# Two attention units in one stretch of TensorE, transposes moved between MLP products, and one fixed list for all operations

## The chip, the cores and the metric

The kernel runs on one core of a Trainium2 chip. The metric is the device time of one execution in microseconds (us), as the median of several runs. Five engines of the core matter: TensorE (PE) multiplies matrices into PSUM, whose banks hold 512 fp32 columns for 128 partitions each; VectorE (DVE), ScalarE (ACT) and GpSimd (POOL) do the arithmetic in between; SyncE (SP) starts the loads and stores. Each engine runs its own list of instructions in order and waits at semaphores for the others.

## The reference

All arrays are fp32: q, k and v of 8 batches, 8 heads, 576 positions and 64 columns; the MLP has 4608 tokens, a model width of 512 and a hidden width of 2048.

```python
scores = scale * np.matmul(q, k.transpose(0, 1, 3, 2))
mask = (rel >= 0) & (rel < window)          # window 128
scores = np.where(mask, scores + bias[None], -1000000000.0)
attn = np.exp(scores - np.max(scores, axis=-1, keepdims=True))
attn = attn / (np.sum(attn, axis=-1, keepdims=True) + 1e-09)
x = np.matmul(attn, v)                      # heads side by side: x is 4608 x 512
h = x @ w_in
P = a[0] + a[1] * h + a[2] * h2 + a[3] * h3
Q = 1.0 + np.abs(b[0]) * np.abs(h) + np.abs(b[1]) * h2
out = (P / (Q + 1e-6)) @ w_out
```

## The kernel before

The 4608 rows are 36 blocks of 128. The attention works on units: one unit is two neighbouring blocks (one in the first two tiles) of one pair of heads. There are 76 units, 8 of them in MLP tile 0 and four in each tile from then on. The MLP works on 18 tiles of 256 tokens and takes the hidden width in chunks of 128, two at a time: up products into a bank h of 512 columns, the rational function on it, down products into two accumulators. Most tiles split each fp32 operand in a high and a low part and multiply three times: `up` (L931) takes w_hi x_hi, w_hi x_lo and w_lo x_hi, `down` (L995) does the same with g_h and g_l.

One unit goes through these steps. `scores` (L537) multiplies queries with keys on quarters of the PE array, 14 products for two usual blocks, into the banks sc0 and sc1 (L552). `softmax` folds the band (L561, DVE), adds the bias and takes the maximum (L568, DVE), and takes the exponential (L573, ACT); `shares` scales by the sum (L585, POOL). Then the weights are transposed on PE, copied to p_all, masked to the two triangles by two selects on POOL (`spread`, L607, L619), and multiplied with v (`quarters`, L641, L650; L742 in the other form). The values come in two halves, into the banks px and py. `sum_halves` (L652) copies the first to x (ACT, L385) and adds the second (DVE, L663); x is cast to x_hi (ACT) and x_lo = x - x_hi is formed (POOL or DVE, L665).

A usual unit has one stretch on PE, made in `attention` (L667): the transposes of the unit before it, in eight halves of 64 rows on parts of the array (`turn_halves`, L593, L598), its own scores, and the values of the unit two before it. `hold`, `pair` and `last_pair` (L758, L778, L809) put two units in one stretch from unit PAIRED on; PAIRED is 76 here, so they are not reached, and the last two units take `turn_alone` (L621, with L591) and the values of L742.

The order of all instructions comes from a planner written in Python. `plan.op` notes an operation with its due time, its cost on each engine that could run it, what it reads and writes. `order` (L182) is a list scheduler over these: it places the ready operation with the earliest due time, with estimated costs (`place`, L249). The list FIRST fixes the order (and by an added 10000 the engine POOL or DVE where there is a choice) of the first 1370 operations. Constants such as ML and ME shift the due times of the down products and of the rational function against the up products. Semaphores are then put in from what the instructions read and write.

Of the kernel before, what the change touches and what calls it, by code (L numbers as in the profile page):

```python
# [140 lines left out]


class Op:
    __slots__ = ("rank", "due", "engines", "emit", "deps", "slots", "left", "users", "start", "end", "engine", "after", "follows", "rows", "sb")
# [985 lines left out]
```

## Time and profile before

| | |
|---|---|
| median of 3 runs | 992.52 us (992.27 to 992.98) |
| the profiled execution | 995.22 us |
| its span, first to last instruction | 993.5 us |
| PE busy | 986.2 us (99%) |
| DVE busy | 769.0 us (77%) |
| ACT busy | 690.6 us (70%) |
| POOL busy | 549.7 us (55%) |
| mean granted clock of PE | 0.997 |

The span is what the profiler saw of the one execution; the 1.7 us beside it lie before its first and after its last instruction. A busy share is the time in which an engine had at least one instruction under way, over the span. Products on PE overlap: one of 512 columns lasts some 0.40 us from its start to its end, while the next begins 0.23 us after it, so the cost of a product in the list is the distance of the starts, not its duration. Line numbers are those of the kernel before.

### The profile page before, as it was taken

Reading aid. Unit: us, or ns where it says so; the run is one execution under the profiler, and the core shown is the slowest. Engines: PE = TensorE matmul, PEld = TensorE weight load, DVE = VectorE, ACT = ScalarE, POOL = GpSimd, SP = SyncE. Lnnn points to the kernel's source line nnn. Section 1 sums busy time; section 2 is a strip of 40 time slices with the busy share of each in tenths; the row PEclk is TensorE's granted clock in tenths of the full one; section 3 lists DMA queues with packets and bytes.
Section 4 is the critical chain, followed back from the end, with each engine's and each line's share of the span. In section 5 each row is a group of like instructions: output and inputs, shape, how many; then the busy total and the mean of one; then the engine's idle time right before and its main releaser. Section 6 shows DMA issues by size and latency. Waiting matters only on the chain.

```text
span 993.5 us, 24565 instructions
## 1 busy us (share of the span) xinstructions
PE 986.2 (99%) x9429; PEld 862.6 (87%) x9431; DVE 769.0 (77%) x1843; ACT 690.6 (70%) x1717; POOL 549.7 (55%) x662
## 2 busy tenths in 40 slices
PE   8999999999999999999999999999999999999998
PEld 5767888888989888898898898988899889898997
DVE  4999988877777877777777877777777777777675
ACT  5999776676767666767667767767666767766563
POOL 3799965555545554545564545455554545454332
PEclk8999999999999999999999999999999999999999
DMA  8973312111212111112111211111111111000000
GB/s 263 342 257 110 105 43 74 44 65 49 71 49 71 44 44 63 56 44 65 54 45 46 74 46 51 66 44 66 53 44 64 55 44 59 37 10 23 1 22 22
DMA packets 45140, 69.08 MB, mean 70 GB/s; under 512 B 4448, under 2 KB 29664, under 8 KB 45024
## 3 DMA queue, kind: packets, MB, share of 16 engines
q1 hardware_dynamic: 44736, 67.26, 20.3%
q8 instruction: 74, 1.21, 0.5%
q14 instruction: 42, 0.34, 0.1%
q10 hardware_dynamic: 288, 0.26, 0.1%
HBM read 58.07 MB, written 9.44 MB: 68 GB/s over the span
## 4 chain that ended last, share of the span: by engine, by line
PE 98%; DMA 1%; SPq 1%; DVE 0%; issue 0%; ACT 0%; ACTq 0%
PE h L931 42%; PE acc L995 42%; PE sc L552 6%; PE px L650 4%; PE px L598 2%; DMA kq<-in_kqv 1%; PE py L650 1%; PE px L742 1%; PE pt L591 0%; PE warm L1051 0%; PE h L937 0%; SPq L486 0%; SPq L844 0%; SPq L487 0%; PE sc L598 0%
## 5 line engine op out<-in xcount | busy, mean ns | idle before, releaser
L931 PE MATMUL h<-x_hi,wi_hi 128*128 128x256 f32 x1024 | 290.9, 284 | 0.0
L931 PE MATMUL h<-x_lo,wi_hi 128*128 128x256 f32 x1024 | 287.9, 281 | 0.0
L931 PE MATMUL h<-x_hi,w_lo 128*128 128x256 f32 x1024 | 287.5, 281 | 0.0
L960 POOL TENSOR_SCALAR g_q<-g_u,babs 128x512 f32<-128x512 f32 x142 | 110.1, 775 | 247.1 <-ACT g_u L959 243.1
L931 PEld LDWEIGHTS h<-x_lo,wi_hi 128*128 128x128 f32 x1024 | 192.6, 188 | 36.3
L995 PE MATMUL acc<-wo_hi,g_h 128*128 128x512 f32 x548 | 220.2, 402 | 0.0
L995 PE MATMUL acc<-w_lo,g_h 128*128 128x512 f32 x548 | 216.3, 395 | 0.0
L931 PEld LDWEIGHTS h<-x_hi,wi_hi 128*128 128x128 f32 x1024 | 193.1, 189 | 23.2 <-issue 1.4
L995 PE MATMUL acc<-wo_hi,g_l 128*128 128x512 f32 x548 | 206.7, 395 | 0.0
L931 PEld LDWEIGHTS h<-x_hi,w_lo 128*128 128x128 f32 x1024 | 193.7, 189 | 0.0
L962 POOL TENSOR_TENSOR g_q<-g_q,g_u 128x512 f32<-128x512 f32 x143 | 185.1, 1295 | 13.8 <-DVE g_q L960 2.9
L965 ACT ACTIVATE g_u<-g_q,guard 128x512 f32<-128x512 f32 x144 | 104.4, 725 | 103.7 <-POOL g_q L962 102.2
L963 DVE TENSOR_TENSOR g_p<-h,g_p 128x512 f32<-128x512 f32 x144 | 99.5, 691 | 90.4 <-ACT g_p L961 88.7
L968 DVE SCALAR_TENSOR_TENSOR g_q<-g_q,h 128x512 f32<-128x512 f32 x144 | 98.7, 685 | 68.3 <-ACT h L967 68.0
L959 ACT ACTIVATE g_u<-h 128x512 f32<-128x512 f32 x141 | 83.9, 595 | 95.8 <-PE h L931 95.7
L619 POOL TENSOR_SCALAR_AFFINE_SELECT p_all<-p_all 128x512 f32<-128x512 f32 (+1 forms) x144 | 90.6, 629 | 69.7 <-ACT p_all L385 61.7
L573 ACT ACTIVATE pr<-pr,st 128x128 f32<-128x128 f32 x288 | 114.7, 403 | 8.1 <-DVE st L568 7.8
L961 ACT ACTIVATE g_p<-h,na 128x512 f32<-128x512 f32 x140 | 108.7, 776 | 0.9 <-PE h L931 0.9
L977 DVE TENSOR_TENSOR g_l<-h,g_h 128x512 fp32r<-128x512 f32 x137 | 93.8, 685 | 19.9 <-ACT g_h L385 19.5
L995 PEld LDWEIGHTS acc<-wo_hi,g_h 128*128 128x128 f32 x548 | 103.2, 188 | 6.2 <-issue 0.7
L964 DVE SCALAR_TENSOR_TENSOR g_p<-g_p,na,h 128x512 f32<-128x512 f32 x144 | 106.8, 742 | 1.8
L969 DVE SCALAR_TENSOR_TENSOR h<-g_p,na,h 128x512 f32<-128x512 f32 x144 | 107.9, 749 | 0.0
(110 smaller groups left out, 1800.2 us busy)
## 6 DMA issues: line engine op xcount, KB each, us to landing
kq<-in_kqv SPq DMA_DIRECT2D x68, 320.0 KB, 3.2
v<-in_kqv SPq DMA_DIRECT2D x68, 192.0 KB, 2.4
out<-o SPq DMA_DIRECT2D x34, 256.0 KB, 2.0
raw_w<-in_w_in SPq DMA_DIRECT2D x16, 512.0 KB, 6.3
raw_w<-in_w_out SPq DMA_DIRECT2D x16, 512.0 KB, 5.2
bias_t<-in_bias SPq DMA_DIRECT2D x44, 64.0 KB, 2.9
kq<-in_kqv SPq DMA_DIRECT2D x4, 192.0 KB, 5.5
kq_first<-in_kqv SPq DMA_DIRECT2D x4, 128.0 KB, 3.0
```

What stands on the lines that cost most here:

```text
L573: nc.scalar.activation(ap(pr)[:, y, :], ap(pr)[:, y, :], AF.Exp, bias=ap(st)[:, y : y + 1], scale=-1.0, accum_out=ap(st)[:, 4 + y : 5 + y])
L931: nc.tensor.matmul(h(i), w[:, k, :], x[:, k, :], start=(k == 0 and m == 0), stop=(k == NKC - 1 and m == len(seq) - 1))
L960: plan.op(E, {"g": tsc, "v": dve(W / 2, 1)} if soon else {"g": tsc}, lambda e: eng[e].tensor_scalar(v(g_q), v(g_u), ap(babs)[:, 1:2], ap(b ...
L961: plan.op(E, either(soon, act(W, 1, 2) - 20, dve(W, 2)), lambda e: nc.scalar.activation(v(g_p), v(h_s), AF.Identity, bias=ap(na)[:, 2:3], ...
L962: plan.op(E, {"g": ttc, "v": dve(W)} if soon else {"g": ttc}, lambda e: eng[e].tensor_tensor(v(g_q), v(g_q), v(g_u), ALU.mult), reads=[(g_ ...
L963: plan.op(E, {"v": dve(W)}, lambda e: nc.vector.tensor_tensor(v(g_p), v(h_s), v(g_p), ALU.mult), reads=[(h_s, 0), (g_p, 0)], writes=[(g_p, ...
L964: plan.op(E, {"v": dve(W, 1)}, lambda e: stt(v(g_p), v(g_p), ap(na)[:, 1:2], v(h_s), ALU.add, ALU.mult), reads=[(h_s, 0), (g_p, 0)], write ...
L965: plan.op(E, {"a": act(W, 0, 1)}, lambda e: nc.scalar.activation(v(g_u), v(g_q), AF.Ln, bias=guard, scale=1.0), reads=[(g_q, 0)], writes=[ ...
L968: plan.op(E, {"v": dve(W)}, lambda e: stt(v(g_q), v(g_q), GUARD, v(h_s), ALU.add, ALU.mult), reads=[(g_q, 0), (h_s, 0)], writes=[(g_q, 0)])
L969: plan.op(E, {"v": dve(W, 1)}, lambda e: stt(v(h_s), v(g_p), ap(na)[:, 0:1], v(h_s), ALU.add, ALU.mult), reads=[(g_p, 0), (h_s, 0)], write ...
L977: plan.op(E, {"v": dve(W)}, lambda e: nc.vector.tensor_tensor(v(g_l), v(h_s), v(g_h).bitcast(F32), ALU.subtract), reads=[(h_s, 0), (g_h, 0 ...
L995: nc.tensor.matmul(ap(accs[n][i]), x[:, sl], w, start=(c == c0 and part == 0 and m == 0), stop=(c == c1 - 1 and (part == 1 or plain) and m ...
```

## The change

PAIRED goes from 76 to 20: from the first unit of the fifth tile on, the 56 units that are left are taken two by two. `pair` makes one stretch of PE for two units. It begins with the values of the two units of the pair before (`emit` in `hold`), into two whole banks px and py, then come the scores of the first unit into sc0 and sc1, as ever, then those of the second (`scores_beside`). These have no bank of their own: four of the fourteen products go to the last quarter of sc0 and sc1, and ten into px and py, after the values there were taken out (`take`: copy of px by ACT or DVE, add of py by DVE, for one unit each). The new argument `glue` holds PE in the planner until the second part of the stretch has followed the first. The transposes of a pair are eight whole ones, an operation of their own (`turn_pair`), and x_hi and x_lo are formed for both units at once (`split` in `hold`, 512 columns). FIRST now names all 6242 operations, so that the due times no longer decide anything; some of the constants are changed as well. The up products of the later tiles wait for the whole x of a tile, as those of the first ones did (`x_reads`).

```diff
-    605, 589, 789, 888, 809, 10855, 856, 810, 606, 791, 788, 793, 811, 10876, 1005, 1351, 812, 10889, 592, 10593, 1007, 10878,
-    890, 1017, 790, 813, 1013, 1010, 891, 792, 816, 910, 1018, 814, 879, 892, 911, 1025, 912, 943, 913, 815, 914, 1019,
...
+    605, 589, 789, 888, 809, 10855, 856, 810, 606, 791, 788, 793, 811, 10876, 1005, 812, 10889, 592, 10593, 1007, 10878, 890,
+    1017, 790, 813, 1013, 1010, 891, 792, 816, 910, 1018, 814, 879, 892, 911, 1025, 912, 943, 913, 815, 914, 1019, 11009,
...
+    6205, 6228, 6230, 6232, 6206, 6229, 6234, 6236, 6235, 6231, 6233, 6238, 6237, 6240, 6239, 6241,
...
+        if glue:
+            glue.glue = o
+            o.deps.add(glue)
...
-                        if r[0] <= t and r[3].engine is None and (best is None or (r[1], r[2]) < (best[1], best[2])) and can(r[3], e, t):
+                        if r[0] <= t and r[3].engine is None and (e != "p" or bound in (None, r[3])) and (best is None or (r[1], r[2]) < (best[1], best[2])) and can(r[3], e, t):
...
-    SA, SG, LL, ML, ZA, ME = 0.082, 0, 6.123, 22.844, 0.779, -17.957
-    OE, CL, CO, WL, SI, SO = -7.408, 4.4, 6.342, -5.815, 31.193, -2.944
-    SL, AW, BL, E0, E1, E2 = -9.614, 22.396, 14.524, 24.893, 13.935, 57.569
+    SA, SG, LL, ML, ZA, ME = 0.082, 0, 6.123, 21.3, 0.779, -24.907
+    OE, CL, CO, WL, SI, SO = -6.174, 4.4, 6.342, -5.815, 31.193, -2.944
+    SL, AW, BL, E0, E1, E2 = -9.614, 41.193, -0.448, 24.893, 13.935, 57.569
...
-    PAIRED, PA, PT, PD, TO, TL, EO, SO2 = 76, -0.35, 6.0, 3.0, 0.0, 0.1, 0.0, 0.0
+    PAIRED, PA, PT, PD, TO, TL, EO, SO2 = 20, -0.205, 1.755, 3.0, 6.604, -4.183, 2.082, 20.604
...
+                part = lambda bank, i, y=y: ap(bank)[:, (2 * y + i) * P : (2 * y + i + 1) * P]
+                c.quarters(lambda i: part(px, i), lambda i: part(py, i))
...
+        def take(at, y):
+            cols = slice(2 * P * y, 2 * P * y + 2 * P)
+            plan.op(at + 0.3, {"a": act(2 * P, 1), "v": dve(2 * P)}, lambda e, y=y: copy(e, ap(x)[:, cols], ap(px)[:, cols]), reads=[(px, y)], writes=[(x, y)], follows=follows)
+            plan.op(at + 0.3, {"v": dve(2 * P)}, lambda e, y=y: nc.vector.tensor_tensor(ap(x)[:, cols], ap(py)[:, cols], ap(x)[:, cols], ALU.add), reads=[(py, y), (x, y)], writes=[(x, y)])
+
+        def split(at):
+            b0 = (STARTS[held[0].j] - MSTART[t]) * P
+            into = lambda y: ap(y)[:, p : p + 2, b0 : b0 + 2 * P]
+            both = lambda: ap(x).rearrange("q (y c) -> q y c", y=2)
+            home = lambda y: [(y, (p + i, held[0].j)) for i in range(2)]
+            mine = [(x, 0), (x, 1)]
+            plan.op(at + 0.4, {"a": act(4 * P, 0), "v": dve(2 * P)}, lambda e: copy(e, into(xh), both()), reads=mine, writes=home(xh), sb=True)
+            plan.op(at + 0.5, {"v": dve(4 * P), "g": 190 + 2.08 * 4 * P}, lambda e: eng[e].tensor_tensor(into(xl), both(), into(xh).bitcast(F32), ALU.subtract), reads=mine + home(xh), writes=home(xl), sb=True)
...
+    def scores_beside(c, sc, late):
+        bank = lambda h: ap(sc[2 + h])
+        spare = lambda h: ap(sc[h])[:, 3 * P :]
+        for i in range(c.m):
...
+                if late == (i == 1 and (n == 1 or c.kinds[i] == 1)):
+                    continue
...
+                            to, k0, k1 = bank(h)[q, : 3 * Q], own - Q, own + P
...
+                        nc.tensor.matmul(to, c.qt(i)[r, q], c.kt(k0, k1)[r], start=True, stop=True, tile_position=(64 * h, Q * half))
...
+    def turn_pair(at):
+        if turning:
+            turning.pop().turn_alone(at, "sc0")
+            return
+        both = pairs[-1]
+        reads = [k for c in both for k in c.turned()]
+        pt = [slot(ps1, [P, 4 * P], F32, "pt", tag=f"sc{y}") for y in range(2)]
+        plan.op(at, {"p": 876}, lambda e: [c.turn([lambda k=k, y=y: ap(pt[y])[:, k * P : (k + 1) * P] for k in range(c.n)]) for y, c in enumerate(both)], reads=reads, writes=[(x, 0) for x in pt])
+        for y, c in enumerate(both):
+            c.spread(at + SO2, pt[y])
...
+        px, py = slot(ps3, [P, 4 * P], F32, "px", tag="h"), slot(ps1, [P, 4 * P], F32, "py", tag="ptx")
+        sc = [slot(ps1, [P, 4 * P], F32, f"sc{k}", tag=f"sc{k}") for k in range(2)] + [px, py]
+        emit, reads, writes, take, split = hold(px, py)
...
+        first = plan.op(A, {"p": 2250}, lambda e: [emit(), both[0].scores(sc[:2]), scores_beside(both[1], sc, False)], reads=reads, writes=writes + [(x, k) for x in sc[:2] for k in range(2)], rows=0.5)
+        first.deps.add(stage[a - 1][0])
+        take(A - 3, 0)
+        o = plan.op(A, {"p": 750}, lambda e: scores_beside(both[1], sc, True), reads=both[1].kq_keys, writes=[(px, 0), (py, 0)], rows=0.5, glue=first)
+        take(A + EO, 1)
+        split(A + EO)
...
-            x_reads = lambda k: x_keys(xs[t], t, range(NKC) if n < EARLY else (k,))
+            x_reads = lambda k: x_keys(xs[t], t, range(NKC) if n < EARLY or first_unit[t] >= PAIRED else (k,))
```

Three places show how the lists of the engines differ. The first is PE where a unit begins, in the list before (x_hi, x_lo and w_lo belong to an up product of the MLP, px, sc0 and sc1 are banks, pr holds a unit's weights, id_sb the identity).

```order
L931 MATMUL h_6223<-x_lo_5038,wi_hi_596 128x256
L931 MATMUL h_6223<-x_hi_5030,w_lo12_1446 128x256
L598 MATMUL px_6246<-id_sb_137,pr_6182 128x64 [waits DVE_49,Pool_49]
L598 MATMUL sc0_6248<-id_sb_137,pr_6182 128x64
L598 MATMUL px_6246<-id_sb_137,pr_6182 128x64 [waits Activation_49]
L598 MATMUL sc0_6248<-id_sb_137,pr_6182 128x64
L598 MATMUL px_6246<-id_sb_137,pr_6182 128x64
L598 MATMUL sc1_6253<-id_sb_137,pr_6182 128x64
L598 MATMUL px_6246<-id_sb_137,pr_6182 128x64 [waits Activation_49]
L598 MATMUL sc1_6253<-id_sb_137,pr_6182 128x64
L552 MATMUL sc0_6248<-kq_5564 64x128 [waits DMAHW6_49]
```

The transposes stood inside the unit's stretch, right ahead of the scores (L552). In the list after, the transposes of a pair of units stand by themselves, some way ahead of the stretch (L1231 are up products, L1295 down products, pt are the banks that they go to):

```order
L1231 MATMUL h_6342<-x_hi_6063,wi_hi_596 128x256
L1231 MATMUL h_6342<-x_lo_6165,wi_hi_596 128x256
L1231 MATMUL h_6342<-x_hi_6063,w_lo4_909 128x256
L817 MATMUL pt_6349<-id_sb_137,pr_6170 128x128 x4
L817 MATMUL pt_6354<-id_sb_137,pr_6167 128x128 x4
L1295 MATMUL acc0_5788<-wo_hi_601,g_l_6264 128x512
L1231 MATMUL h_6342<-x_hi_6063,wi_hi_596 128x256
L1231 MATMUL h_6342<-x_lo_6165,wi_hi_596 128x256
L1231 MATMUL h_6342<-x_hi_6063,w_lo4_909 128x256
```

Eight whole transposes take the place of the eight halves of each of two units, and MLP products stand on both sides. The second place is PE at the end of a stretch, before:

```order
L650 MATMUL py_6269<-p_all_6155,v_5558 64x128 [waits PE_49]
L650 MATMUL py_6269<-p_all_6155,v_5558 64x128
L650 MATMUL px_6246<-p_all_6155,v_5558 64x64 x2
L650 MATMUL py_6269<-p_all_6155,v_5558 64x64 x2
L650 MATMUL px_6246<-p_all_6155,v_5558 64x128 x2
L650 MATMUL py_6269<-p_all_6155,v_5558 64x128 x2
L650 MATMUL px_6246<-p_all_6155,v_5558 64x64 x2
L650 MATMUL py_6269<-p_all_6155,v_5558 64x64 x2
L931 MATMUL h_6223<-x_hi_5030,wi_hi_596 128x256
L931 MATMUL h_6223<-x_lo_5038,wi_hi_596 128x256
```

The stretch ended with values products, and the next instructions of the MLP carried no wait. The same place after, in the stretch of two units (kq holds queries and keys; L1045 is `scores_beside`):

```order
L1045 MATMUL sc1_5394<-kq_5099 64x128
L1045 MATMUL px_5358<-kq_5099 64x2x64 [waits Activation_49]
L1045 MATMUL py_5361<-kq_5099 64x2x64 [waits DVE_49]
L1045 MATMUL px_5358<-kq_5099 64x192
L1045 MATMUL py_5361<-kq_5099 64x192
L1045 MATMUL px_5358<-kq_5099 64x64
L1045 MATMUL py_5361<-kq_5099 64x64
L1045 MATMUL px_5358<-kq_5099 64x64
L1045 MATMUL py_5361<-kq_5099 64x64
L1045 MATMUL px_5358<-kq_5099 64x64
L1045 MATMUL py_5361<-kq_5099 64x64
L1295 MATMUL acc0_5155<-wo_hi_601,g_l_5354 128x512
```

The stretch now ends with scores of the second unit, and the first that go to px and py carry a wait each, for ACT and for DVE; what they wait for are the copy and the add that take the values out. The third place is ACT at such an eviction. Before (g_u, g_p, g_h and h belong to the rational function, x to a unit):

```order
L385 COPY p_all_5878<-sc0_5825 128x2x64 [waits DVE_49]
L967 ACTIVATE h_5739<-g_u_5812 128x512 [waits Activation_49]
L385 COPY p_all_5878<-sc1_5830 128x2x64 [waits DVE_49,PE_49]
L385 COPY p_all_5878<-px_5823 128x4x64 [waits PE_49]
L385 COPY x_5900<-px_5823 128x256
L573 ACTIVATE pr_5884,st_5885<-pr_5884,st_5885 128x128 x2
L385 CAST x_hi_5766<-x_5900 128x256 [waits DVE_49]
L573 ACTIVATE pr_5884,st_5885<-pr_5884,st_5885 128x128
L959 ACTIVATE g_u_5921<-h_5800 128x512 [waits PE_49]
```

The copy of px stood behind three copies of transposes and ahead of exponentials (L573). After, for the same stretch as above:

```order
L1267 ACTIVATE h_5181<-g_u_5243 128x512 [waits DVE_49,Activation_49]
L1259 ACTIVATE g_u_5308<-h_5214 128x512 [waits PE_49]
L1261 ACTIVATE g_p_5337<-h_5214,na_489 128x512
L611 CAST g_h_5351<-h_5181 128x512 [waits DVE_49]
L611 COPY x_pair_5415<-px_5358 128x256 [waits PE_49]
L1265 ACTIVATE g_u_5308<-g_q_5329,guard_74 128x512 [waits Activation_49,Pool_49]
L1267 ACTIVATE h_5214<-g_u_5308 128x512 [waits DVE_49,Activation_49]
```

One copy of x_pair stands between a cast of g_h and a logarithm (L1265); the other half is copied elsewhere. In four stretches both copies are ACT's, with another instruction between them, as here:

```order
L611 CAST g_h_3927<-h_3736 128x512 [waits DVE_49]
L1259 ACTIVATE g_u_3949<-h_3865 128x512 [waits PE_49]
L611 COPY x_pair_4006<-px_3954 128x256 [waits PE_49]
L611 CAST g_h_4008<-h_3786 128x512 [waits DVE_49]
L611 COPY x_pair_4006<-px_3954 128x256
L1261 ACTIVATE g_p_4014<-h_3865,na_489 128x512
```

The cast of g_h, which waits for DVE, now stands between the two copies of one eviction.

## Rows read from the trace of the kernel before

**Rows 1.** The page: busy line, and the clock in its 40 slices.

```profile
PE 986.2 (99%) x9429; PEld 862.6 (87%) x9431; DVE 769.0 (77%) x1843; ACT 690.6 (70%) x1717; POOL 549.7 (55%) x662
...
PEclk8999999999999999999999999999999999999999
...
PE 98%; DMA 1%; SPq 1%; DVE 0%; issue 0%; ACT 0%; ACTq 0%
```

**Rows 2.** The waits of PE: us in total, times, longest us.

```profile
PE sc L552 <- DMA kq<-in_kqv: 1.4, 1, 1.4
```

**Rows 3.** One stretch: busy of PE, PEld, DVE, ACT, POOL; clock, DMA share, GB/s.

```profile
400.00:453.40 53.40, 53.40 (x539) 48.07 (x538) 40.13 (x99) 36.99 (x96) 28.39 (x35) 1.00 0.16 53
```

**Rows 4.** Timeline of PE at a unit: start us, duration us, instruction.

```profile
404.25 0.40 PE L995 MATMUL acc<-wo_hi,g_l 128*128 128x512 f32 x1
404.58 0.27 PE L598 MATMUL px<-id_sb,pr 64*128 64x64 f32 x1
...
404.97 0.94 PE L552 MATMUL sc<-kq 64*64 64x128 f32 x24
405.69 0.27 PE L650 MATMUL px<-p_all,v 64*64 64x128 f32 x1
...
406.36 0.22 PE L650 MATMUL py<-p_all,v 64*64 64x64 f32 x1
406.51 0.50 PE L995 MATMUL acc<-wo_hi,g_h 128*128 128x512 f32 x1
406.84 0.39 PE L995 MATMUL acc<-w_lo,g_h 128*128 128x512 f32 x1
407.07 0.40 PE L995 MATMUL acc<-wo_hi,g_h 128*128 128x512 f32 x1
```

**Rows 5.** Timeline of PE at the last stretch of scores and values.

```profile
894.88 0.28 PE L931 MATMUL h<-x_hi,w_lo 128*128 128x256 f32 x1
...
896.85 0.28 PE L931 MATMUL h<-x_lo,wi_hi 128*128 128x256 f32 x1
```

**Rows 6.** Timeline of PE at four transposes between MLP products.

```profile
909.13 0.39 PE L995 MATMUL acc<-wo_hi,g_l 128*128 128x512 f32 x1
...
909.92 0.28 PE L931 MATMUL h<-x_lo,wi_hi 128*128 128x256 f32 x1
```

**Rows 7.** Timeline of PE at values by themselves.

```profile
905.09 0.40 PE L995 MATMUL acc<-wo_hi,g_l 128*128 128x512 f32 x1
...
906.66 0.28 PE L931 MATMUL h<-x_lo,wi_hi 128*128 128x256 f32 x1
```

**Rows 8.** Timeline of PE and ACT where the values are taken out.

```profile
896.47 0.22 PE L650 MATMUL px<-p_all,v 64*64 64x64 f32 x1
...
896.72 0.37 ACT L385 COPY x<-px 128x256 f32<-128x256 f32 x1
```

**Rows 9.** The instructions on x: count, ns shortest/median/longest, first and last start, form.

```profile
L385 ACT COPY x<-px x63: 350/383/427, 34.7 to 896.7; 128x256 f32<-128x256 f32 x63
L663 DVE TENSOR_TENSOR x<-py,x x62: 406/418/427, 103.8 to 897.3; 128x256 f32<-128x256 f32 x62
```

**Rows 10.** Timeline of ACT and DVE in the rational function.

```profile
411.56 0.59 ACT L385 CAST g_h<-h 128x512 fp32r<-128x512 f32 x1 [0.90 <-DVE h L975]
...
412.18 0.69 DVE L977 TENSOR_TENSOR g_l<-h,g_h 128x512 fp32r<-128x512 f32 x1 [0.58 <-ACT g_h L385]
```

**Rows 11.** Timeline of DVE and PE where PE waits for DVE.

```profile
27.14 0.28 DVE L385 COPY x_plain<-px 128x128 f32<-128x128 f32 x1
...
27.48 0.49 PE L937 MATMUL h<-x_plain,w 128*128 128x128 f32 x2
```

**Rows 12.** Groups of POOL: busy us, mean ns of one, idle before and its releasers.

```profile
L962 POOL TENSOR_TENSOR g_q<-g_q,g_u 128x512 f32<-128x512 f32 x143 | 185.1, 1295 | 13.8 <-DVE g_q L960 2.9
L960 POOL TENSOR_SCALAR g_q<-g_u,babs 128x512 f32<-128x512 f32 x142 | 110.1, 775 | 247.1 <-ACT g_u L959 243.1 <-DVE h L969 3.8
...
L619 POOL TENSOR_SCALAR_AFFINE_SELECT p_all<-p_all 128x512 f32<-128x512 f32 x136 | 87.3, 642 | 67.1 <-ACT p_all L385 60.6 <-DVE o L1036 1.9
```

More of the change, by code (lines that the diff above doesn't have):

```diff
@@ L143 @@
 class Op:
-    __slots__ = ("rank", "due", "engines", "emit", "deps", "slots", "left", "users", "start", "end", "engine", "after", "follows", "rows", "sb")
+    __slots__ = ("rank", "due", "engines", "emit", "deps", "slots", "left", "users", "start", "end", "engine", "after", "follows", "rows", "sb", "glue")
 class Plan:
@@ L756, in banded_attention_ratio_mlp, with hold @@
     pairs = []
-    def hold(at, sc, deps):
+    def hold(px, py):
         held = [x["unit"] for x in waiting[:2]]
         del waiting[:2]
-        bank = slot(ps3, [P, 4 * P], F32, "px", tag="h")
-        if len(sc) == 1:
-            second = lambda y, i: ap(sc[0])[:, (2 * y + i) * P : (2 * y + i + 1) * P]
-            others = lambda y: [(0, 2, lambda: ap(sc[0])[:, 2 * y * P : (2 * y + 2) * P], [(sc[0], 1)])]
-        else:
-            second = lambda y, i: ap(sc[2 * y + i])[:, 3 * P :]
-            others = lambda y: [(i, i + 1, lambda i=i: ap(sc[2 * y + i])[:, 3 * P :], [(sc[2 * y + i], 1)]) for i in range(2)]
@@ new lines, in hold @@
+        reads = [k for c in held for k in c.v_keys + [(c.w, 0), (c.w, 1)]]
+        return emit, reads, [(b, y) for b in (px, py) for y in range(2)], take, split
+    def scores_beside(c, sc, late):
+        bank = lambda h: ap(sc[2 + h])
+        spare = lambda h: ap(sc[h])[:, 3 * P :]
+        for i in range(c.m):
+            own = (i + 1) * P
+            for n in range(2):
+                if late == (i == 1 and (n == 1 or c.kinds[i] == 1)):
+                    continue
+                for half in range(2):
+                    q = slice(Q * half, Q * half + Q)
+                    if n and not i and (half or c.kinds[i] == 1):
+                        continue
+                    if i and c.kinds[i] == 1 and n:
+                        continue
+                    for h in range(2):
+                        if c.kinds[i] == 1:
+                            to, k0, k1 = (spare(h) if i else bank(h)[:, Q : 3 * Q])[q], own, own + P
+                        elif not i and half:
+                            to, k0, k1 = bank(h)[q, : 3 * Q], own - Q, own + P
+                        elif not i and n:
+                            to, k0, k1 = bank(h)[q, Q : 2 * Q], own, own + Q
+                        elif not i:
+                            to, k0, k1 = bank(h)[q, : 3 * Q].rearrange("q (k c) -> q k c", c=Q)[:, ::2], own - P, own
+                        elif n:
+                            to = spare(h)[q] if half else spare(h)[q].rearrange("q (k c) -> q k c", c=Q)[:, ::-1]
+                            k0, k1 = (own, own + P) if half else (own - Q, own + Q)
+                        else:
+                            to, k0, k1 = bank(h)[q, 3 * Q : 4 * Q], own - Q if half else own - P, own if half else own - Q
+                        r = slice(64 * h, 64 * h + 64)
+                        nc.tensor.matmul(to, c.qt(i)[r, q], c.kt(k0, k1)[r], start=True, stop=True, tile_position=(64 * h, Q * half))
@@ L791, in pair @@
             reads = reads + c.kq_keys
-            cost += c.price - 55
-        o = plan.op(A, {"p": SESSION + cost}, lambda e: [emit(), both[0].scores(sc[:2]), both[1].scores(sc[2:])], reads=reads, writes=writes + [(x, 0) for x in sc], rows=0.5)
-        o.deps.add(stage[a - 1][0])
-        evict(A + EO)
+        first = plan.op(A, {"p": 2250}, lambda e: [emit(), both[0].scores(sc[:2]), scores_beside(both[1], sc, False)], reads=reads, writes=writes + [(x, k) for x in sc[:2] for k in range(2)], rows=0.5)
[4 more added lines that the diff above has]
+        split(A + EO)
         stage[a] = stage[a + 1] = [o]
@@ L810, in last_pair @@
         A = p_time(len(units))
-        for y, c in enumerate(pairs[-1]):
-            c.turn_alone(A - PT + PD * y, f"sc{y}")
-        sc = [slot(ps1, [P, 4 * P], F32, "py", tag="ptx")]
-        emit, reads, writes, cost, evict = hold(A, sc, None)
-        plan.op(A, {"p": SESSION + cost}, lambda e: emit(), reads=reads, writes=writes, rows=0.5)
-        evict(A)
+        turn_pair(A - PT)
+        px, py = slot(ps3, [P, 4 * P], F32, "px", tag="h"), slot(ps1, [P, 4 * P], F32, "py", tag="ptx")
+        emit, reads, writes, take, split = hold(px, py)
+        plan.op(A, {"p": 1520}, lambda e: emit(), reads=reads, writes=writes, rows=0.5)
+        take(A, 0)
+        take(A, 1)
+        split(A)
     def x_keys(slots, t, ks, js=None):
```

50 lines of the change are left out of this document (33 added, 17 removed), and 264 rows, old and new, of the table FIRST.

## The prediction, made before the change was run

> **What bounds the kernel now.** I read the page's busy line and its slices first. TensorE (PE) is busy 986.2 of 993.5 us, the granted clock stands at its full level (2.4 GHz) after the first slice, and the chain that ended last is PE for 98% [rows 1]. The reader is to see that there is hardly any idle time to win: PE itself waited only at the start, once 1.4 us for a load and below 1 us for the rest [rows 2]. In the stretch that computes one MLP tile, 400 to 453.4 us, PE is busy for all 53.40 us, VectorE (DVE) for 40.13, ScalarE (ACT) for 36.99 and GpSimd (POOL) for 28.39 [rows 3]. So the time is the length of PE's own list, and a change can win only by shortening that list and lose only by making PE wait. Nothing waits now: every wait that the change adds is paid in full.
>
> What one attention unit costs in the list is read from the timeline around 404 us [rows 4]. The last MLP product before it starts at 404.25, the second one behind it at 406.84: 2.59 us, less two products of 512 columns, which follow each other by 0.23 (406.84 to 407.07): 2.12 us for the unit. Of this 0.10 is the way in (404.25 + 0.23 to 404.58), 0.39 the eight half transposes (to 404.97), 0.72 the scores (to 405.69), 0.72 the values products (to 406.36 and a step of 0.05), 0.09 the way out (to 406.51), and 0.10 the first MLP product, which takes 0.33 to the next in place of 0.23. A stretch of scores and values alone shows the same pieces: 894.88 to 896.85 is 1.97, less two products of 0.12, 1.73 us [rows 5].
>
> **What the change takes away.** 55 such units and five smaller pieces at the end become 28 stretches for two units each, 28 groups of eight whole transposes between MLP products, one group of four, and one stretch of values alone. A stretch for two costs, if nothing waits, 0.10 + 4 x 0.72 + 0.09 + 0.10 = 3.17; it ends on scores, not on values, so I take 3.20. Four whole transposes between MLP products are in the trace: 909.13 to 909.92 is 0.79, less 0.23 and 0.12, 0.44 us, and no way in or out is paid there [rows 6]. For eight I take 0.88 (bounds 0.78, if the way in, 0.10 in [rows 4], is paid once, and 0.88). Two units cost 4.24 before and 4.08 now: 0.16 saved, 28 times, 4.5 us. At the end stood two groups of four transposes (0.88), a stretch of 1.73 and two of values at 1.22 (905.09 to 906.66 is 1.57, less 0.23 and 0.12) [rows 7], 5.05 in all. In their place come the 56th unit, which is in the 28 pairs (2.12), four transposes (0.44) and one stretch of values (about 1.73): 0.76 saved. Together 5.2 us; I let it lie between 3 and 7. That 12 blocks begin a sequence and need fewer products is the same on both sides.
>
> ACT, DVE and POOL issue fewer and longer instructions: one copy of a whole bank for three, one cast and one subtraction for two units. I cost this at nothing either way, since each has over 13 us to spare in a tile [rows 3]. The loads move on SP's queue, but DMA engines are busy 0.16 of that tile [rows 3], and I cost this at nothing too.
>
> **What it adds: a wait inside the stretch.** The second unit's scores go into the banks px and py, which hold the values of the two units before. The order shows the first of them on PE waiting for ACT (px) and for DVE (py). In the built program the first half's copy, though it reads only the first unit's columns, waits for the last px product of the second unit, and the add of py for the last py product. So the chain starts only when all 64 values products are through. Its links are in the trace: from the start of the last px product to ACT's copy 0.25 (896.47 to 896.72) [rows 8], the copy 0.38 [rows 9], to DVE 0.03 (411.56 + 0.59 to 412.18) [rows 10], the add 0.42 [rows 9], and to PE 0.06 (27.14 + 0.28 to 27.48) [rows 11]: 1.14 us. PE has in the meantime a step of 0.05, the first unit's scores, 0.72, and four of the second unit's fourteen rows, a third of its streamed columns, 0.24: 1.01. It then waits 0.13 us with both engines free, in each of 28 stretches: 3.6 us. Behind the wait stand the rest of the scores and the whole MLP list; everyone waits.
>
> In six stretches the order has more in the chain. In four, ACT's copy of the other half, with one cast or activation of some 0.59 ahead of it [rows 10], stands before the point that PE waits for: 0.25 + 0.38 + 0.59 + 0.38 + 0.06 = 1.66, 0.52 more than 1.14. In one DVE does copy, add and copy (0.43 more), and in one a subtraction of 0.69 stands between them as well (1.1 more). That is 4 x 0.52 + 0.43 + 1.1 = 3.6 us. In six others three or four DVE operations of the MLP, 0.69 each like the one in [rows 10], stand between the last one that opens the stretch and the eviction. If they start with the stretch, three end 2.1 us after it, and the eviction could begin at 1.64 (64 values products, 1.39, and 0.25): up to 0.45 late. I take half of 6 x 0.45, 1.4 us; the bounds of the whole wait are 0 and 28 x 1.0 (one operation ahead on each engine).
>
> Here a rule speaks on the change. The Trainium skill, PSUM — Partial Sum Buffer, section "PSUM bank collisions raise a hardware error", says that accesses of two engines are to be guarded by bank, not by address. The program's waits agree with it; no run here shows what a guard by address would give. By address the chain would start 0.72 us earlier and be over before PE arrives, and the sum would be the savings alone, about 987.3 us; by bank it is the sum below.
>
> **What else may be late.** The values of a pair follow their transposes by 4.4 to 8 us of PE's list (they had over 9 before). Between stand ACT's two copies of a whole bank, which I put at the 0.59 of the cast in [rows 10], and four selects on POOL at 0.64 [rows 12]. The first copy starts 0.25 after the transposes [rows 8], and 0.25 + 0.59 + 4 x 0.64 = 3.4 us if POOL is free. With one MLP pair of 0.775 and 1.295 on POOL ahead of them [rows 12] it is 5.5, and the second unit's values, which come 0.72 later, would be up to 0.4 late in the tightest places, more where ACT is late too. I take 0, and keep 0 to 0.7 per pair for it (0 to 20 us).
>
> **The sum.** The profiled execution took 995.22 us, its span 993.5 and 1.7 around it. 995.2 - 5.2 + 3.6 + 3.6 + 1.4 = 998.6. The median of the runs shown is 2.7 below the profiled one: 995.9 us.
>
> **The rivals.**
> 1. The wait hides (faster). If PE takes slightly longer to the second unit's scores than 1.01, or the links are shorter by the same 0.13, only the crowded stretches wait. For it: both sums differ by 0.13 only. Against it: the six stretches with more in the chain. 992.5 - 5.2 + 1.5 = 988.8 us. It decides where the chain is below 1.0 us.
> 2. They cancel (no change). The 0.13 is paid 28 times, the crowded queues turn out to be free: 992.5 - 5.2 + 3.6 + 1.5 = 992.4 us. For it: DVE and ACT are free a quarter and a third of the tile.
> 3. The values wait for POOL, or an h product for a bank that the pair holds longer, on top of the forecast: 0.5 us in each of 28 pairs, 14 us: 1010 us. For it: the distance of 4.4 us. Against it: POOL is idle for 25 us of a tile [rows 3].
>
> **Chances.** The forecast, 993.5 to 1001 us, 0.40; rival 1 0.23; rival 2 0.22; rival 3 0.15. About 0.2% is what a measurement of this kernel can tell from no change: below 990.5 lies rival 1 and a little of rival 2 (0.25), within 990.5 to 994.5 most of rival 2 and the lower end of the forecast (0.25), above it the rest (0.50). The range of 8 in 10 reaches from the savings with little of the waits, 988, to rival 3 short of its middle, 1007.
>
> **What would show it.** In the profile after, transposes between MLP products of about 0.88 us, and stretches of 3.2 us without a wait, show the savings right. In the waits of PE's weight loads, px and py products at the new scores line waiting for ACT and DVE copies and adds of x_pair, some 0.1 to 0.3 us each and 0.6 and more in six, show the loss right; none there makes rival 1. Waits of the values products for POOL's selects would show rival 3. A PE busy below 980 us with an idle share spread over the MLP would mean that I missed the place. A granted clock under its full level after a stretch would prove the whole sum wrong.

## The result, and the profile after

The changed kernel takes 998.0 us (median of 4 runs, 997.45 to 999.18) against 992.75 us of the kernel before beside it: a ratio of 1.0054, with a 95% interval of 1.0037 to 1.0072. It is slower, by 5.25 us. The forecast was 995.9 us.

The page of the profiled execution (999.18 us, span 997.5), to be held against [rows 1]:

```profile
PE 985.1 (99%) x9345; PEld 864.3 (87%) x9347; DVE 782.9 (78%) x1917; ACT 666.5 (67%) x1548; POOL 550.7 (55%) x637
...
PEclk9999999999999999999999999999999999999999
...
PE 87%; DVE 4%; DMA 4%; ACT 2%; issue 1%; SPq 1%; POOL 0%; DVEq 0%; ACTq 0%
```

PE was busy 1.1 us less and the span is 4.0 us longer, and the chain that ended last, 98% PE before, now goes through DVE, ACT and loads for a tenth of its length. The waits of PE (engine, line, what it waited for: us in total, times, longest) against [rows 2]:

```profile
PE px L1045 <- DVE x_pair L611: 1.5, 2, 1.0
PE px L1045 <- ACT x_pair L611: 1.2, 4, 0.3
...
PE acc L1295 <- ACT g_h L611: 0.6, 1, 0.6
...
PE h L1231 <- DVE x_lo L1011: 0.3, 1, 0.3
```

This view names the place, the scores that go to px (L1045), but only its six crowded stretches: a wait that falls between products that still overlap leaves PE busy, and is not listed. So the timeline has to be read, by starts. First the eight transposes between MLP products, to be held against [rows 6]:

```profile
387.24 0.39 PE L1295 MATMUL acc<-w_lo,g_h 128*128 128x512 f32 x1
387.47 1.03 PE L817 MATMUL pt<-id_sb,pr 128*128 128x128 f32 x8
388.26 0.37 PE L1231 MATMUL h<-x_hi,wi_hi 128*128 128x256 f32 x1
388.47 0.28 PE L1231 MATMUL h<-x_lo,wi_hi 128*128 128x256 f32 x1
```

From 387.24 to 388.47 is 1.23; less 0.23 and 0.12 that is 0.88 us, as predicted. A stretch in which ACT copies px, on the timeline of PE, ACT and DVE:

```profile
395.15 0.40 PE L1295 MATMUL acc<-w_lo,g_h 128*128 128x512 f32 x1
395.48 0.33 PE L876 MATMUL px<-p_all,v 64*64 64x128 f32 x2
...
396.81 0.23 PE L876 MATMUL px<-p_all,v 64*64 64x64 f32 x2
...
396.86 0.90 PE L778 MATMUL sc<-kq 64*64 64x128 f32 x24
397.08 0.37 ACT L611 COPY x_pair<-px 128x256 f32<-128x256 f32 x1 [2.90 <-PE py L876]
...
397.48 0.42 DVE L1002 TENSOR_TENSOR x_pair<-py,x_pair 128x256 f32<-128x256 f32 x1 [2.58 <-ACT x_pair L611]
397.53 0.45 PE L1045 MATMUL sc<-kq 64*64 64x128 f32 x8
397.75 0.38 PE L1045 MATMUL px<-kq 64*64 64x128 f32 x2
...
397.96 0.32 PE L1045 MATMUL py<-kq 64*64 64x128 f32 x1
...
398.55 0.73 PE L1295 MATMUL acc<-wo_hi,g_l 128*128 128x512 f32 x2
```

The copy starts 0.26 after the last px product, although its columns were written 0.67 before it; the add follows, ends at 397.90, and the first py product starts at 397.96. Its neighbour of px, issued 0.01 ahead of it wherever nothing waits, stands at 397.75. So PE loses 0.20 us here. In 15 of the 28 stretches DVE makes the copy too, as at 744.6:

```profile
745.92 0.22 PE L876 MATMUL px<-p_all,v 64*64 64x64 f32 x2
...
746.19 0.42 DVE L611 COPY x_pair<-px 128x256 f32<-128x256 f32 x1 [1.06 <-PE py L876]
...
746.72 0.42 DVE L1002 TENSOR_TENSOR x_pair<-py,x_pair 128x256 f32<-128x256 f32 x1
746.87 0.38 PE L1045 MATMUL px<-kq 64*64 64x128 f32 x2
...
747.06 0.68 DVE L1277 TENSOR_TENSOR g_l<-h,g_h 128x512 fp32r<-128x512 f32 x1
...
747.20 0.32 PE L1045 MATMUL py<-kq 64*64 64x128 f32 x1
```

Here the copy takes 0.05 more than ACT's, the add starts 0.11 after it in place of 0.03, and px to py is 0.33: PE loses 0.32. The worst of the crowded stretches, at 557.2:

```profile
558.80 0.42 DVE L611 COPY x_pair<-px 128x256 f32<-128x256 f32 x1 [1.61 <-PE py L876]
...
559.33 0.42 DVE L1002 TENSOR_TENSOR x_pair<-py,x_pair 128x256 f32<-128x256 f32 x1
...
559.67 0.68 DVE L1277 TENSOR_TENSOR g_l<-h,g_h 128x512 fp32r<-128x512 f32 x1
...
560.27 0.41 DVE L611 COPY x_pair<-px 128x256 f32<-128x256 f32 x1
...
560.74 0.32 PE L1045 MATMUL px<-kq 64*64 64x128 f32 x1 [1.03 <-DVE x_pair L611]
```

The px product waits for the second copy, which nothing in its columns asks for, and g_l stands between. Read so, by the place of the first late py product in each stretch, the 28 waits add up to 10.6 us.

To see where the rest went, I take the starts of PE's products from the 417th up product to the last MLP product, the same list of MLP work in every kernel, and count what lies between MLP products as the attention's, and what MLP products follow each other later than in the kernel before as MLP waits. (The 417th is counted in L931, L1231 after. Up to it the profiled executions of this case differ by some 4 us, 162.8 to 167.0, much as their starts do; in these two it comes at 165.7 and 164.5.)

| us of PE's list | before | after |
|---|---|---|
| attention: stretches and transposes | 118.8 | 121.1 |
| MLP waits | 0 | 2.6 |
| 417th up product to the last product | 823.6 | 828.6 |

Two of the MLP waits are large, 0.60 and 0.86 us with the longer step behind them: an up product waits for x_lo, and a down product for ACT's cast of g_h.

```profile
195.64 0.69 DVE L1011 TENSOR_TENSOR x_lo<-x_pair,x_hi 128x512 fp32r<-128x512 f32 x1 [0.48 <-ACT x_hi L611]
...
195.78 0.28 PE L1231 MATMUL h<-x_hi,wi_hi 128*128 128x256 f32 x1
...
196.39 0.39 PE L1231 MATMUL h<-x_lo,wi_hi 128*128 128x256 f32 x1 [0.33 <-DVE x_lo L1011]
...
728.57 0.28 PE L1231 MATMUL h<-x_hi,w_lo 128*128 128x256 f32 x1
...
728.80 0.59 ACT L611 CAST g_h<-h 128x512 fp32r<-128x512 f32 x1 [1.10 <-DVE h L1275]
...
729.44 0.50 PE L1295 MATMUL acc<-wo_hi,g_h 128*128 128x512 f32 x1 [0.60 <-ACT g_h L611]
```

The other 1.1 us are pieces of 0.1 to 0.5, nearly all at up products; the largest, 0.51 at 935.1, waits for the copies of px in the last stretch of values, whose bank is one of the banks h.

### The profile page after: what moved, and what is told of

The parts are those of the page before. It is cut to its first block, busy times and chain, and to the rows that moved or that the text cites. A ratio compares the mean times of both kernels' runs of the same rounds, so it can differ in the third digit from the quotient of the medians.

```text
span 997.5 us, 24310 instructions
## 1 busy us (share of the span) xinstructions
PE 985.1 (99%) x9345; PEld 864.3 (87%) x9347; DVE 782.9 (78%) x1917; ACT 666.5 (67%) x1548; POOL 550.7 (55%) x637
## 4 chain that ended last, share of the span: by engine, by line
PE 87%; DVE 4%; DMA 4%; ACT 2%; issue 1%; SPq 1%; POOL 0%; DVEq 0%; ACTq 0%
PE acc L1295 38%; PE h L1231 38%; PE px L876 4%; PE pt L817 2%; PE sc L778 2%; DMA raw_w<-in_w_in 2%; DMA kq<-in_kqv 1%; PE px L1045 1%; PE py L1045 1%; PE py L876 1%; DVE w L1157 1%; DMA v<-in_kqv 1%; DMA raw_w<-in_w_out 1%; PE sc L1045 1%; DVE g_q L1268 0%
## 5 line engine op out<-in xcount | busy, mean ns | idle before, releaser
L1231 PE MATMUL h<-x_hi,wi_hi 128*128 128x256 f32 x1024 | 290.9, 284 | 0.4 <-DVE x_pair L611 0.3
L1231 PE MATMUL h<-x_lo,wi_hi 128*128 128x256 f32 x1024 | 287.8, 281 | 0.3 <-DVE x_lo L1011 0.3
L1231 PE MATMUL h<-x_hi,w_lo 128*128 128x256 f32 x1024 | 287.4, 281 | 0.0
L1295 PE MATMUL acc<-wo_hi,g_h 128*128 128x512 f32 x548 | 218.6, 399 | 0.6 <-ACT g_h L611 0.6
L1295 PE MATMUL acc<-w_lo,g_h 128*128 128x512 f32 x548 | 216.1, 394 | 0.0
L1231 PEld LDWEIGHTS h<-x_lo,wi_hi 128*128 128x128 f32 x1024 | 193.2, 189 | 21.9 <-DVE x_lo L1011 0.5
L1231 PEld LDWEIGHTS h<-x_hi,wi_hi 128*128 128x128 f32 x1024 | 192.8, 188 | 18.9 <-issue 1.1
L1295 PE MATMUL acc<-wo_hi,g_l 128*128 128x512 f32 x548 | 205.8, 397 | 0.0
L1231 PEld LDWEIGHTS h<-x_hi,w_lo 128*128 128x128 f32 x1024 | 193.7, 189 | 0.0
L1265 ACT ACTIVATE g_u<-g_q,guard 128x512 f32<-128x512 f32 x144 | 104.3, 724 | 36.5 <-POOL g_q L1262 36.1
L611 ACT CAST g_h<-h 128x512 fp32r<-128x512 f32 x135 | 79.1, 586 | 63.8 <-DVE h L1275 62.4
L1295 PEld LDWEIGHTS acc<-w_lo,g_h 128*128 128x128 f32 x548 | 103.4, 189 | 11.4 <-issue 0.5
L1295 PEld LDWEIGHTS acc<-wo_hi,g_h 128*128 128x128 f32 x548 | 103.2, 188 | 9.7 <-ACT g_h L611 1.1
L1295 PEld LDWEIGHTS acc<-wo_hi,g_l 128*128 128x128 f32 x548 | 101.0, 188 | 11.6
L1267 ACT ACTIVATE h<-g_u 128x512 f32<-128x512 f32 x144 | 86.5, 601 | 33.2 <-DVE g_p L1264 30.9
```

The costliest lines, as they stand in the source:

```text
L611: (nc.scalar.copy if e == "a" else eng[e].tensor_copy)(out, src)
L1231: nc.tensor.matmul(h(i), w[:, k, :], x[:, k, :], start=(k == 0 and m == 0), stop=(k == NKC - 1 and m == len(seq) - 1))
L1265: plan.op(E, {"a": act(W, 0, 1)}, lambda e: nc.scalar.activation(v(g_u), v(g_q), AF.Ln, bias=guard, scale=1.0), reads=[(g_q, 0)], writes=[ ...
L1267: plan.op(E, {"a": act(W, 0)}, lambda e: nc.scalar.activation(v(h_s), v(g_u), AF.Exp, scale=-1.0), reads=[(g_u, 0)], writes=[(h_s, 0)])
L1295: nc.tensor.matmul(ap(accs[n][i]), x[:, sl], w, start=(c == c0 and part == 0 and m == 0), stop=(c == c1 - 1 and (part == 1 or plain) and m ...
```

## Experiments

The ratio is to the kernel before on the same chip, to be held against the change's 1.0054. Theory A is that PE waits for the eviction of px and py. Of each edit the telling lines are shown; three dots stand for the rest.

**No wait in the stretch.** The late scores go over sc0 and sc1:

```diff
     def scores_beside(c, sc, late):
-        bank = lambda h: ap(sc[2 + h])
+        bank = lambda h: ap(sc[h])
```

> The ten late products of a pair's second unit go to sc0 and sc1, over the scores of its first unit, in place of px and py (so the attention of 56 units is computed from wrong scores; nothing is left out). PE issues the same products, but nothing in the stretch waits for the copy or the add. Theory A (the waits in the 28 stretches, read as first late py product minus its place behind the early products, add up to 10.6 us, and two units cost 3.08 without them): 998.0 - 10.6 = 987.4 us, full stretches of 3.08 us from 3.28 to 3.59. Rival B (two units cost the 3.20 of the prediction, the waits are 7.5 us): 990.5 us, full stretches of 3.20. Rival C (the loss lies in the order of the MLP's work, the stretch only shows it): 995 us or more, with new waits of up or down products.

Measured: 995.32 us, ratio 1.0017 (1.0007 to 1.0026). The time is rival C's, but the stretches are theory A's: ten full ones cost 3.06 to 3.12 us, so that 3.20 was too much. 13 others wait right behind the stretch, by 0.2 to 0.6 us, as at 583.5 (timeline of this run):

```profile
585.63 0.42 DVE L1002 TENSOR_TENSOR x_pair<-py,x_pair 128x256 f32<-128x256 f32 x1
...
585.97 0.68 DVE L1277 TENSOR_TENSOR g_l<-h,g_h 128x512 fp32r<-128x512 f32 x1
...
586.71 0.39 PE L1231 MATMUL h<-x_hi,wi_hi 128*128 128x256 f32 x1 [0.27 <-DVE g_l L1277]
```

The next up product needs a bank h. One of the three holds px, and the one that is due is freed by g_l, which DVE does only after copy and add. With the wait behind it, this stretch costs 3.40 us, what it cost in the changed kernel: two waits for DVE ended there at the same time, and taking one away uncovered the other. (Three more stretches wait 0.6 to 1.3 us for banks that this edit itself overwrites.)

**The second half later.**

```diff
+            for o in (c1, a1):
+                c = next(c for c in codes if c % 10000 == w[o])
+                if codes.index(c) < codes.index(w[late]):
+                    codes.remove(c)
+                    codes.insert(codes.index(w[late]) + 1 + (o is a1), c)
...
```

Here c1 and a1 are copy and add of the second unit held.

> In the fixed list the copy and the add of the second unit held are moved behind the late scores in all pairs, so that PE waits in no stretch for more than the first half of the eviction; the order on ACT and DVE stays. Theory A: the six crowded stretches (3.59 four times, 3.74, 4.34) fall to 3.28 and 3.40: 4 x 0.31 + 0.34 + 0.93 = 2.5 us, 995.5 us. Rival B (ACT and DVE are just as late for the MLP's products behind the stretch, so the time is waited for there): 997 to 998 us with new waits of down products for g_h or g_l.

Measured: 998.67 us, ratio 1.0047 (1.0035 to 1.006), not to be told from the change. The stretch at 557.2 fell from 4.34 to 3.40 and the crowded others to between 3.27 and 3.44; attention is 1.7 us shorter, MLP waits 0.9 longer. Theory A held in the stretches, rival B in about half of the time: half of what PE no longer waits for there, it waits for later.

**The early scores twice.**

```diff
-... lambda e: [emit(), both[0].scores(sc[:2]), scores_beside(both[1], sc, False)], ...
+... lambda e: [emit(), both[0].scores(sc[:2]), scores_beside(both[1], sc, False), scores_beside(both[1], sc, False)], ...
```

> The four early products of the second unit are issued twice, one set right behind the other (same result). PE's own work in a full stretch grows by 0.22 us, 25 to 28 times, about 5.7 us in all. Theory A (PE waits there at least 0.19 to 0.32 us anyway): the extra work falls into the wait, stretches of 3.28 rise to 3.31, those of 3.40 and above stay: 998.0 to 999 us. Rival B (the time between the early and the late products is PE's own, not a wait): 998.0 + 5.7 = 1003.7 us.

Measured: 999.1 us, ratio 1.0057 (1.0044 to 1.007). Attention is 121.2 us in place of 121.1: of the 5.7 us of more work on PE that were expected nothing is seen. That part of the stretch is waiting, as theory A has it.

**Two copies side by side, put first.** The add of the two halves then on DVE:

```diff
+            for o in (a0, c0):
+                c = next(c for c in codes if c % 10000 == w[o])
+                codes.remove(c)
+                codes.insert(codes.index(w[first]) + 1, w[o])
...
+                return c, plan.op(at + 0.3, {"v": dve(2 * P)}, lambda e: nc.vector.tensor_copy(half(), ap(py)[:, cols]), ...
```

> The first half of an eviction is taken out by two copies side by side, px by ACT and py by DVE, both put right behind the stretch's first part in the list; the sum of the two is formed later on DVE, before the add of the second half; the second half is moved behind the late scores as well (same result). Theory A: from the last values product 0.26 + 0.42 + 0.06 = 0.74 us until PE may go on, it arrives after 0.94: no wait where both engines are free, full stretches of 3.08 us. 28 more additions of 256 columns on DVE (11.8 us, busy 78 to 79%). If ACT and DVE are free everywhere 998.0 - 10.6 = 987.4; I expect some stretches with ACT or DVE busy at that point, 988 to 991 us. Rival B (another instruction on ACT or DVE is under way at that point in most stretches, or the moved ones delay the MLP): 993 to 998 us.

Measured: 1006.48 us, ratio 1.0132 (1.0118 to 1.0146). Inside the stretches the wait was gone nearly everywhere, but attention stayed at 120.9 us, since twelve of them now waited behind their end, and the MLP waits rose to 11.4. The third stretch is one of the twelve. On ACT's timeline, first of the changed kernel, where it begins at 236.6, then of this run, where it begins at 235.2:

```profile
237.23 0.59 ACT L611 CAST g_h<-h 128x512 fp32r<-128x512 f32 x1 [0.85 <-DVE h L1275]
...
236.55 0.37 ACT L623 COPY x_pair<-px 128x256 f32<-128x256 f32 x1 [3.00 <-PE py L888]
...
237.97 0.59 ACT L623 CAST g_h<-h 128x512 fp32r<-128x512 f32 x1
```

The cast of g_h, 0.6 behind the start of the stretch before, now stands behind the copy that waits for PE, 2.8 behind the start, and everything after it (g_l, the bank h) comes later. A wait put to the front of an engine's list delays what is ready behind it. The run also gives DVE 28 additions more, and how much of the loss is theirs isn't shown.

**The bank h freed earlier.** Three kernels and a control, in which the result of the rational function goes to SBUF:

```diff
-            plan.op(E, {"v": dve(W)}, lambda e: stt(v(h_s), v(g_q), 2.0, v(h_s), ALU.subtract, ALU.mult), ...
+                rooms.append(rooms[-1] if rooms else slot(const, [P, 2, 512], F32, "g", tag="raw"))
...
+            plan.op(E, {"v": dve(W)}, lambda e: stt(g(h_s), v(g_q), 2.0, v(h_s), ALU.subtract, ALU.mult), ...
```

> The run in which the late scores go over the first unit's scores in sc0 and sc1 (attention of 56 units from wrong scores, nothing left out), and besides, from the fifth tile on, the result of the rational function is written to SBUF in place of the bank h, so that the cast of g_h and the subtraction of g_l no longer hold that bank. Theory A (two bounds lie one behind the other: PE waits for the eviction in the stretch, and right behind it for the h bank, which g_l holds while DVE does the eviction first): the 4.4 us of waits behind the stretches and most of the 2 to 3 us of waits for g_l inside the MLP go, 995.3 - 6 = 989 us. Rival B (DVE as a whole is late there, whichever bank it frees): the up products' waits turn into waits of down products for g_l or g_h, 994 us or more.

> The changed kernel with the second half of the eviction behind the late scores, and the result of the rational function written to SBUF from the fifth tile on (same output). Theory A: stretches stay at 3.28 and 3.40, since they wait for the eviction; only the waits of up products for the h bank inside the MLP (about 1.5 us) go: 996.5 to 997.5 us. Rival B (the h bank is the bound everywhere): 993 us or less. Rival C (the cast and the subtraction are slower from SBUF): 998 us or more.

> The eviction of the first half by two copies side by side (px by ACT, py by DVE), each placed in the list where its engine is free in the trace of the changed kernel; the sum of the two on POOL; the second half behind the late scores; the result of the rational function in SBUF from the fifth tile on (same output). Theory A (both bounds are met): full stretches of 3.08 in most pairs, few waits behind them: 998.0 - 10.6 + 2 to 3 = 990 us, faster than the kernel before. Rival B (POOL or ACT takes the place of DVE, or DVE stays late): 994 us or more, with waits of values products for POOL or of up products for DVE.

> The kernel before, with the result of the rational function written to SBUF from the fifth tile on (same output). Theory A (before the change no bank h was waited for, its trace shows no wait in the MLP): within 0.2% of the kernel before. Rival B (the bank h held PE there too, hidden in the product times): 990 us or less.

Measured: 994.83 (ratio 1.0014, 1.0005 to 1.0023), 1000.02 (1.0058, 1.0044 to 1.0072), 998.53 (1.0047, 1.0033 to 1.006) and, for the control, 997.01 us (1.0032, 1.002 to 1.0045): the numbers of the rivals B and C. In the control both theories failed: the edit costs the kernel before some 3 us. A reason that can be read from the traces is that of rival C, a slower subtraction. Here it is in the control, and last in the second of the three (count, ns shortest/median/longest, first and last start), with h in PSUM up to the fourth tile and g in SBUF after it:

```profile
L982 DVE TENSOR_TENSOR g_l<-g,g_h x112: 682/1073/1501, 256.5 to 987.8; 128x512 fp32r<-128x512 f32 x112
L982 DVE TENSOR_TENSOR g_l<-h,g_h x25: 658/684/693, 90.3 to 250.5; 128x512 fp32r<-128x512 f32 x25
...
L1290 DVE TENSOR_TENSOR g_l<-g,g_h x112: 661/728/1823, 263.0 to 992.2; 128x512 fp32r<-128x512 f32 x112
```

With both inputs in SBUF the median is 1.07 us in the control and 0.73 in the other run, in place of 0.68, and the longest take 1.5 and 1.8. The length goes with POOL: the 14 in the control beside which POOL has nothing under way take 0.68 to 0.69, the 72 beside which it is busy for over 60% of the time have a median of 1.30. With h in PSUM POOL makes no difference. The Trainium skill, SBUF — State Buffer, section "Who interferes with whom", says that a DVE instruction with two SBUF inputs contends with a GpSimd instruction that reads SBUF, and that one with at most one such input, outside DVE's 2-port modes, does not; the rows agree. In the control the planner also orders anew all but the operations that FIRST names: from the 417th up product on, PE goes 892 times straight from an up to a down product, in the kernel before 818 times. So its 3 us are not shown to be the subtraction's alone, and these runs tell nothing of the bank h by itself.

**Two copies where the engines are free, the sum on POOL.**

```diff
+            def second(e):
+                nc.gpsimd.tensor_tensor(one(), half(), one(), ALU.add)
+                copy(e, ap(x)[:, cols], ap(px)[:, cols])
...
```

A list AHEAD says how many of ACT's and DVE's next operations stay ahead of each pair's copies.

> The changed kernel with the result of the rational function in the bank h, as it was, and the eviction of the first half by two copies side by side (px by ACT, py by DVE), each put in the list where its engine is free in the trace of the changed kernel; their sum on POOL; the second half behind the late scores (same output). DVE then does one copy of 0.42 where it did a copy and an add or waited for ACT's copy, so the subtraction for g_l behind it, which frees the bank h, starts 0.43 earlier where DVE did both. Theory A (the eviction, and DVE's work behind it, make the loss): full stretches of 3.08 in most pairs, 998.0 - 10.6 + about 3 for the pairs in which ACT is busy = 990 to 991 us. Rival B (the sum on POOL, both of whose inputs lie in SBUF, holds up DVE's operations on SBUF or the selects): 994 us or more, with DVE operations of over 1 us beside it.

Measured: 995.39 us, ratio 1.0018 (1.0007 to 1.0029). Attention is 113.6 us, 7.5 less than in the change, 14 full stretches cost 3.06 to 3.07; but MLP waits are 7.6. Theory A held for the stretches, not for the time. The largest of what is left lies behind a few pairs: 1.0 us for ACT's copy of o, which the list put behind the copy of px, and twice about 1 us for a softmax on px or sc.

**Without the first unit's adds.**

```diff
-... lambda e, y=y: nc.vector.tensor_tensor(ap(x)[:, cols], ap(py)[:, cols], ap(x)[:, cols], ALU.add), ...
+... lambda e, y=y: y and nc.vector.tensor_tensor(ap(x)[:, cols], ap(py)[:, cols], ap(x)[:, cols], ALU.add), ...
...
```

The second half stands behind the late scores here too, as in the run "The second half later".

```diff
+                    codes.insert(codes.index(w[late]) + 1 + (o is a1), c)
```

> The changed kernel with the second half of the eviction behind the late scores, and without the 29 adds of py for the first unit held (its values are those of one half of the keys, a part of the attention of 29 units is left out). PE waits for the copy of px alone: 1.34 + 0.26 + 0.38 to 0.43 + 0.06 = 2.04 to 2.09, and arrives at 2.28. Theory A: no wait in the stretch (3.08), and 0.42 less on DVE ahead of g_l, so little wait behind it: 998.0 - 10.6 + 1 to 2 = 988 to 989 us. Rival B (what PE waits for behind the stretch is not DVE's eviction): 993 us or more with up products waiting for g_l as in the run with the late scores over sc0 and sc1.

Measured: 989.97 us, ratio 0.997 (0.9961 to 0.9979). From the run "The second half later" (1.0047) it differs by one DVE add of 0.42 us per pair, 29 in all, and nothing else; without them the kernel is faster than before, with them slower. A stretch of it on PE's timeline:

```profile
391.62 0.40 PE L1303 MATMUL acc<-w_lo,g_h 128*128 128x512 f32 x1
...
393.33 0.90 PE L786 MATMUL sc<-kq 64*64 64x128 f32 x24
394.00 0.45 PE L1053 MATMUL sc<-kq 64*64 64x128 f32 x8
...
394.81 0.73 PE L1303 MATMUL acc<-wo_hi,g_l 128*128 128x512 f32 x2
```

From the early scores to the next MLP product is 0.81 us, where the changed kernel took 1.02 with ACT's copy (397.53 to 398.55). Attention is 111.1 us, 10.0 less than in the change, and only three stretches wait 0.2 to 0.4 behind their end. Theory A's number was 1 to 2 us too low. The wait in the stretch and the one right behind it go together, with the add on DVE; rival B is out. The MLP waits further on do not go with it: they are 3.6 us, and 3.5 in that run.

**Each pair as it goes best.** The run before last, with copy and add kept in six pairs:

```diff
+KEEP = 1, 11, 12, 18, 22, 23
...
-        beside = slot(sb2, [P, 2, P], F32, "x") if held[0].u < 74 else None
+        beside = slot(sb2, [P, 2, P], F32, "x") if (held[0].u - 18) // 2 not in KEEP + (28,) else None
...
```

> The run with two copies and their sum on POOL, but in six of the 28 pairs (the 2nd, 12th, 13th, 19th, 23rd and 24th), where it cost 0.1 to 1.1 us more from one stretch to the next than copy and add, copy and add stay, with the second half behind the late scores (same output). Theory A (the pairs stand for themselves): the six give back 0.06 + 0.28 + 0.14 + 0.75 + 1.01 + 1.06 = 3.3 us, 995.4 - 3.3 = 992.1 us, ratio to the kernel before 0.9985. Rival B (what one pair saves the next one waits for): 994 us or more, ratio 1.001 or more.

Measured: 991.71 us, ratio 0.9981 (0.9971 to 0.999). That is theory A's number (0.9985). This version leaves nothing out; it is 0.2% faster than the kernel before and some 0.7% (0.9981 over 1.0054) faster than the change; attention is 113.4 us, MLP waits 4.4.

## Why the prediction was right

- **The bound and the direction.** PE's list was full, and the wait that the change adds is paid in full, by the place and the order of events that the prediction named: last px product, copy, add, first late product. Shown by the timeline, and by three runs: twice the early work cost nothing, taking the wait away gave 3.07 us in ten full stretches, taking the add away gave the time back.
- **The savings were sized too low.** Predicted 5.2 us (3 to 7); the run without adds has 118.8 - 111.1 = 7.7, with about 1 us of waits still in it, and so over the stated bound. The transposes are right (0.88). The stretch for two is 3.07 and not 3.20: the term 4 x 0.72 took each part as it lies in one unit's stretch, but scores ahead of other scores take 0.67 (393.33 to 394.00).
- **The waits too, by 1.4 to 2.0 us.** Predicted 8.6 us; measured 10.6 by the timeline, 10.0 by the run without adds. The links were right (0.26, 0.37, 0.03, 0.42, 0.06). Mis-sized was the first 3.6: it took ACT's copy and 0.13 for all stretches. With scores at 0.67, PE arrives earlier, and the wait is 0.20 with ACT's copy. In 15 stretches DVE makes the copy, the chain is 0.13 longer, and the wait is 0.32. Where a block begins a sequence, PE has less to do in between and waits 0.3 to 0.44. The order showed which engine copies, so this could have been counted. The six crowded stretches were sized at 3.6 and cost 1.24 + 0.34 + 0.93 = 2.5 above the others. The 1.4 for DVE being late was wrong: in no stretch did a copy by DVE start later than 0.32 us after the last px product.
- **The errors partly cancel**: attention was forecast to grow by 3.4 us, and it grew by 2.3, with savings and waits both too low; the MLP waits bring the sum to 4.9. That the forecast is only 2.1 us off is in part luck.
- **What it left out.** 2.6 us of MLP waits behind the stretches, put at nothing. At most 1.1 of them are of rival 3's kind ("an h product for a bank that the pair holds longer"); the rest are the waits for g_h and x_lo shown above, which no rival named. The values of the pairs waited for POOL nowhere: the one stretch that began late (0.19, at 637.6) did so 0.7 after POOL's last select had ended.
- **Rivals 1 and 2** lived on a wait of no more than 0.13 us; in full stretches it was 0.20 and more.
- **The rule on banks.** The copy starts after the last product on its bank, in all 28 stretches, in a full one 0.9 us after the last product for its own columns, and so the sum by bank held; no run guarded by address.

Open: how much of the loss is the bank h alone. The run without the wait shows that bank to be the next bound behind DVE's eviction; every run that freed it earlier also slowed subtractions on DVE. What makes the 2.6 us of MLP waits was read from the timeline, and no run took them away. The cost of the transposes' new place, apart from all else, wasn't tried.

## What to carry to other kernels

When two pieces of work share a bank, as px and py do here, expect the second to wait for the whole eviction of the first: add up copy, add and hand-overs and compare with what the waiting engine has left to do, for each engine that may do the copy. Before taking such a wait away, look at what the evicting engine does next and who needs that; here, in 13 of 28 stretches, the subtraction behind the eviction was due at the same moment, and the time came back only where the engine also had less to do before it. A copy put early in an in-order list helps only if nothing behind it could have run before.

## What the runs showed of the hardware

- A subtraction of 512 columns on DVE takes 0.66 to 0.69 us with one input in PSUM, whatever POOL does. With both in SBUF it takes 0.68 to 0.69 beside an idle POOL and, beside a busy one, 1.30 in the middle and up to 1.50 (the control; up to 1.82 in the three others).
- From a DVE copy to a DVE add that needs it 0.11 us pass (746.61 to 746.72), from an ACT copy to the same add 0.03: one engine working behind itself was slower than a hand-over.
- The scores of a unit take 0.67 us of PE ahead of other scores, 0.72 ahead of values products. (They are 12 products in the usual form, 14 in the second; the text ahead of the prediction gave 14 for both.)
